# Splitting a sequence transform into even and odd tokens, on row and column tiles of TensorE

## The chip, the cores and the metric

The kernel runs on one core of one Trainium2 chip. The metric is the device time of that core in microseconds (us), the median of several executions. A profile is of one execution, and its span is 1.8 us shorter than that execution's own time (206.0 against 207.83 us in the kernel before). "The stretch" below is the time from the start of the first feed-forward matmul to the start of the last. The engines are TensorE (PE in the profile, PEld its weight loads), VectorE (DVE), ScalarE (ACT), GpSimd (POOL) and SyncE (SP). SP does no arithmetic here; it only starts the DMA transfers, and the profile calls that work SPq.

## The reference, cut to what matters

```python
B, H, S, D = 4, 8, 768, 48
def attn(r, k, v, w, u):                 # per batch and head, token by token
    for t in range(S):
        y[t]  = r[t] @ (state + outer(u * k[t], v[t]))
        state = w[t][:, None] * state + outer(k[t], v[t])

x = y.transpose(0, 2, 1, 3).reshape(4, 768, 384)
mixed = real(fft(fft(x, axis=1), axis=2))        # axis 1: tokens, axis 2: features
u  = x + mixed
un = (u - mean(u)) / sqrt(var(u) + 1e-6)         # layer norm over the features
out = u + relu(un @ w_ch1) @ w_ch2               # 384 -> 1536 -> 384
```

All inputs and the output are fp32. The change concerns the two transforms, and with them the order in which tokens lie on the partitions of the on-chip memory.

## The kernel before

The program is written as a list of operations with dependencies. A small list scheduler in the kernel file gives each engine its static order and sets the semaphores between engines. Attention works in 24 chunks (4 batches of 6) of 128 tokens; a chunk needs four loads (w, k, r, v). Each load is one DMA that puts 128 tokens on 128 partitions, in 1,024 pieces of 192 bytes (8 heads of 48 fp32 for each token):

```python
def load(b, c):
    for n in "wkrv":
        def f(e, n=n, i=i):
            return e.dma_start(INB[n][i][:, :, :],
                               src[n][b, :, c*CH:(c+1)*CH, :].rearrange("h t d -> t h d"))
        op("sp", 60, f, ..., sem="in_%s%d" % (n, i), nbytes=CH * DM * 4)
```

The first transform (over tokens) takes the sums and differences `xf` of mirrored features, and multiplies them by cosine and sine tables for 385 frequencies. The second (over features) multiplies the result by further tables. Both use the full array of 128 rows by 128 columns. A row tile is a part of this array that takes only some of the rows (input partitions), a column tile one that takes only some of the columns (output partitions); a mode change is a passage from one such division to another. The feed-forward part follows, batch by batch, while the next batches' attention runs:

```python
for s in range(NC):                      # first transform: 24 matmuls of 385 columns per batch
    e.matmul(ps(t)[:, 0:HF], xf[:, s, off:off+128], tab[:, s, :], start=a, stop=z)
...
for j in range(3):                       # second transform: 18 matmuls of 384 columns per batch
    lt = hcs[:, j, 128*kb:128*kb+128] if kb < 3 else hcr[:, j, 128*kb-S//2 : 128*kb-S//2+128]
    e.matmul(ps(t)[:, 0:DM], lt, dt[:, j, :], start=(j == 0), stop=(j == 2))
...
for q in range(HP):                      # attention product: already on two row tiles
    for x in range(2):
        e.matmul(ps(ta[x])[:, 128*q:128*q+128], kT[64*x:64*x+D, q, :], rT[64*x:64*x+D, q, :])
...
e.matmul(ps(t)[:, 0:384], W1[:, m, 128*j:128*j+128], unt[:, m, :], ...)   # feed-forward, first half
e.matmul(ps(t)[:, 0:DM], ht[:, j, 128*x:128*x+128], W2[:, j, :], ...)     # feed-forward, second half
e.dma_start(out[b, kb*128:(kb+1)*128, :], o[:, :])                        # 24 stores of 192 KB
```

## Time and profile before

| | before |
|---|---|
| median time (4 runs: 208.38 to 210.4) | 208.91 us |
| span of the profiled execution | 206.0 us |
| first feed-forward matmul | 53.9 us |
| last input landed / last attention product | 118.9 / 163 us |
| last matmul started | 202.6 us |
| TensorE busy between 53.9 and 202.9 | 148.5 of 149.0 us |

The first lines are from the page of the kernel before. Each digit of PE and DMA is the busy share of one fortieth of the span, in tenths; GB/s is what the DMA engines moved in that slice.

```profile
PE   1298887799899999999999999999999999999993
...
DMA  5999999399699999999999810011110200211202
GB/s 124 220 210 210 181 217 219 49 187 203 110 222 178 219 188 215 214 216 224 205 256 249 182 46 0 0 41 38 38 43 0 80 0 0 81 38 38 76 23 94
```

But for two dips, DMA is full until just past the middle, and TensorE is full from the twelfth slice on. Next comes the chain of waits that ended last, in shares of the span by engine.

```profile
PE 80%; DVE 8%; POOL 5%; DMA 2%; ACT 2%; issue 2%; SPq 1%; ACTq 0%; DVEq 0%; POOLq 0%
```

TensorE alone carries four fifths of it; the DMA issues (SPq) have 1%. The table of stretches (length, then each engine's busy time and number of instructions, the clock granted to TensorE, the busy share of the DMA engines, GB/s) makes the same point with numbers:

```profile
0.00:53.90 53.90, 39.91 (x405) 23.44 (x406) 43.03 (x120) 39.45 (x82) 37.90 (x49) 1.00 0.95 180
53.90:202.90 149.00, 148.53 (x1354) 94.38 (x1354) 104.24 (x228) 105.17 (x242) 71.92 (x88) 1.00 0.49 111
202.90:206.00 3.10, 0.00 (x1) 0.00 (x0) 0.62 (x1) 0.00 (x0) 0.00 (x0) 1.00 0.24 85
```

From 53.9 us on, TensorE has half a microsecond of idle time in 149. The time is therefore the start (53.9) plus what TensorE must do after it (149) plus a tail of 3 us.

Last, TensorE's timeline around an attention product (line L613) between two groups of full-array matmuls:

```profile
73.47 0.81 PE L758 MATMUL bank<-w,ht 128*128 128x384 bf16 x4
74.22 0.40 PE L613 MATMUL bank<-rtb,ktb 48*128 48x128 bf16 x8
74.54 0.34 PE L682 MATMUL bank<-ss,xf 128*128 128x385 bf16 x1
```

Four matmuls of 384 columns, 162 ns apart, would let the next one start at 74.12; it starts at 74.22. So the change from the full array to row tiles costs just under 100 ns. The records give 258 ns instead of 162 on the way in and 148 instead of 56 on the way out: 92 to 96 ns per change.

### The profile page before, as it was taken

To read this page: it belongs to the slowest core of one execution; us is meant where nothing else is said; L and a number is where in the kernel's file an instruction comes from. 1 tells how busy PE (TensorE), PEld (TensorE's weight loads), DVE (VectorE), ACT (ScalarE), POOL (GpSimd) and SP (SyncE) were. 2 spreads that over 40 slices of the span, in tenths; PEclk is the share of its full clock that TensorE was granted. 3 is DMA by queue.
4 is the path that set the end of the run, shared out by engine and by line. 5 is a ranking of instruction groups with operands and counts; after the bars stand their busy time and mean duration, and the time that the engine had idled before them with its cause. 6 is when DMAs were issued, how large, how long until landed. Compare 5 with 4: busy or idle time off the path is not lost.

```text
span 206.0 us, 4594 instructions
## 1 busy us (share of the span) xinstructions
PE 188.4 (91%) x1758; PEld 117.8 (57%) x1758; DVE 147.9 (72%) x348; ACT 144.6 (70%) x322; POOL 109.8 (53%) x136
## 2 busy tenths in 40 slices
PE   1298887799899999999999999999999999999993
PEld 0164553446565666666667666666666666665661
DVE  8917989859987878499878974999778338622222
ACT  5979987474988898868886759689963463881420
POOL 2396895779256987892798887813542130000000
PEclk9999999999999999999999999999999999999999
DMA  5999999399699999999999810011110200211202
GB/s 124 220 210 210 181 217 219 49 187 203 110 222 178 219 188 215 214 216 224 205 256 249 182 46 0 0 41 38 38 43 0 80 0 0 81 38 38 76 23 94
DMA packets 105414, 26.45 MB, mean 128 GB/s; under 512 B 100272, under 2 KB 105008, under 8 KB 105392
## 3 DMA queue, kind: packets, MB, share of 16 engines
q1 hardware_dynamic: 103440, 23.80, 53.4%
q0 software_dynamic: 1952, 2.36, 7.0%
q8 instruction: 14, 0.23, 0.4%
q14 instruction: 8, 0.07, 0.1%
HBM read 23.79 MB, written 4.72 MB: 138 GB/s over the span
## 4 chain that ended last, share of the span: by engine, by line
PE 80%; DVE 8%; POOL 5%; DMA 2%; ACT 2%; issue 2%; SPq 1%; ACTq 0%; DVEq 0%; POOLq 0%
PE bank L739 23%; PE bank L758 23%; PE bank L682 7%; PE bank L698 6%; PE bank L613 3%; POOL rk L398 2%; DMA in_v<-in_v_dram 2%; PE bank L594 2%; PE bank L715 2%; PE bank L600 2%; DVE ah L618 2%; PE bank L553 2%; PE bank L651 2%; PE bank L557 2%; PE bank L801 1%
## 5 line engine op out<-in xcount | busy, mean ns | idle before, releaser
L739 PE MATMUL bank<-unt,w 128*128 128x384 bf16 x288 | 54.8, 326 | 0.2 <-ACT unt L720 0.2
L758 PE MATMUL bank<-w,ht 128*128 128x384 bf16 x288 | 54.0, 326 | 0.0
L748 ACT ACTIVATE ht<-bank 128x384 bf16<-128x384 f32 x80 | 38.1, 490 | 17.0 <-PE bank L739 16.6
L618 DVE TENSOR_TENSOR ah<-bank,msk 128x512 bf16<-128x512 f32 x48 | 31.3, 682 | 6.2 <-PE bank L613 5.9
L758 PEld LDWEIGHTS bank<-w,ht 128*128 128x128 bf16 x288 | 26.9, 98 | 15.4
L739 PEld LDWEIGHTS bank<-unt,w 128*128 128x128 bf16 x288 | 26.2, 97 | 15.7 <-issue 0.4
L398 POOL TENSOR_TENSOR rk<-in_r,in_k 128x384 f32<-128x384 f32 x24 | 24.2, 1013 | 10.2 <-DMA in_r<-in_r_dram 9.1
L398 POOL TENSOR_TENSOR xf<-x 128x191 bf16<-128x191 f32 x18 | 11.4, 632 | 30.1 <-DVE x L657 30.1
L763 DVE SCALAR_TENSOR_TENSOR osb<-bank,rstd,uf 128x384 f32<-128x384 f32 x24 | 14.7, 614 | 17.6 <-PE bank L758 17.4
L398 POOL TENSOR_TENSOR vtd<-in_v,dc 128x384 f32<-128x384 f32 x24 | 19.9, 832 | 9.8 <-DVE dc L575 9.6
L398 POOL TENSOR_TENSOR rk<-rk,ub 128x384 f32<-128x384 f32 x24 | 24.0, 1005 | 0.3
L603 ACT ACTIVATE rtb<-bank 128x512 bf16<-128x512 bf16 x24 | 14.3, 594 | 6.8 <-PE bank L594 6.0
L412 ACT ACTIVATE un<-uf,agg 128x384 bf16<-128x384 f32 x24 | 14.2, 608 | 5.9 <-DVE agg L706 5.9
L605 ACT ACTIVATE ktb<-bank 128x512 bf16<-128x512 bf16 x24 | 14.3, 595 | 4.3 <-PE bank L600 4.1
L412 ACT ACTIVATE vb<-in_v 128x384 bf16<-128x384 f32 x24 | 12.5, 522 | 5.6 <-DMA in_v<-in_v_dram 3.0
L657 DVE TENSOR_TENSOR x<-bank,vtd 128x384 f32<-128x384 f32 x24 | 13.3, 553 | 4.4 <-PE bank L651 4.2
L744 DVE TENSOR_SCALAR ht<-bank 128x384 bf16<-128x384 f32 x16 | 8.8, 552 | 10.2 <-PE bank L739 10.2
L583 DVE TENSOR_TENSOR rh<-bank,in_r 128x384 bf16<-128x384 f32 x24 | 13.2, 551 | 3.0 <-ACT bank L559 2.7
L700 DVE TENSOR_TENSOR uf<-bank,x 128x384 f32<-128x384 f32 x24 | 12.6, 543 | 3.1 <-PE bank L698 2.8
L801 PE MATMUL bank<-idw,msk 128*128 128x384 bf16 x48 | 12.0, 353 | 3.0 <-DVE idw L402 3.0
L720 ACT ACTIVATE unt<-bank 128x384 bf16<-128x384 f32 x24 | 11.6, 491 | 4.0 <-PE bank L715 3.7
L553 PE MATMUL bank<-lb,msk 128*128 128x384 bf16 x24 | 8.2, 342 | 6.4 <-ACT lb L412 5.0
(100 smaller groups left out, 364.2 us busy)
## 6 DMA issues: line engine op xcount, KB each, us to landing
in_w<-in_w_dram SPq DMA_DIRECT2D x24, 192.0 KB, 3.8
in_k<-in_k_dram SPq DMA_DIRECT2D x24, 192.0 KB, 3.8
in_r<-in_r_dram SPq DMA_DIRECT2D x24, 192.0 KB, 3.8
in_v<-in_v_dram SPq DMA_DIRECT2D x24, 192.0 KB, 3.9
out_dram<-osb SPq DMA_DIRECT2D x24, 192.0 KB, 1.9
w<-in_moe_w_ch_dram POOLq DMA_DIRECT2D x2, 1152.0 KB, 11.7
ub<-in_u_dram SPq DMA_DIRECT2D x1, 192.0 KB, 3.8
```

The lines of the kernel that those rows point to most:

```text
L398: return shared(lambda e: e.tensor_tensor(out=o, in0=a, in1=b, op=f))
L412: return lambda e: e.activation(o, a, f, **kw)
L603: op("act", 570, lambda e: e.activation(rT[:, :, :].rearrange("p h t -> p (h t)"), psb(trr)[:, 0:512], ACTF.Copy), r=[trr], w=[("RTB", i2)])
L605: op("act", 570, lambda e: e.activation(kT[:, :, :].rearrange("p h t -> p (h t)"), psb(trk)[:, 0:512], ACTF.Copy), r=[trk], w=[("KTB", i2)])
L618: masked[n] = op("dve", 660, lambda e, x=x: e.tensor_tensor(out=ah[:, x:H:2, :], in0=ps(ta[x])[:, :].rearrange("p (h t) -> p h t", t=128), ...
L657: op("dve", 530, lambda e: e.tensor_tensor(out=xb[:, c, 0:DM], in0=ps(ty)[:, 0:DM], in1=vtd[:, :, :].rearrange("t h d -> t (h d)"), op=ALU ...
L682: return e.matmul(ps(t)[:, 0:HF], xf[:, s, off:off + 128], tab[:, s, :], start=a, stop=z)
L739: ins = e.matmul(ps(t)[:, 0:384], W1[:, m, 128 * j:128 * j + 128], unt[:, m, :], start=(m == 0), stop=(m == NM - 1))
L748: op("act", 475, lambda e, j=j, t=t, ht=ht: e.activation(ht[:, j, :], ps(t)[:, 0:384], ACTF.Relu), r=[t], w=[("HT", q % 2, j)])
L758: ins = e.matmul(ps(t)[:, 0:DM], ht[:, j, 128 * x:128 * x + 128], W2[:, j, :], start=(j == 0), stop=(j == NJ - 1))
L763: op("dve", 610, lambda e, kb=kb, t=t, o=o: e.scalar_tensor_tensor(out=o[:, :], in0=ps(t)[:, 0:DM], scalar=rstd[:, kb:kb + 1], in1=uf[:, k ...
L801: ins = e.matmul(ps(tw)[:, 0:384], MSK[:, :], IDW[:, :])
```

## The change

The transform of 768 tokens is split into even and odd tokens. Each half sum runs on half of the rows: even tokens lie on partitions 0 to 63 and odd tokens on 64 to 127, and two matmuls of 64 rows by 193 columns run side by side on two row tiles. For the frequencies k and 384 - k the two half sums are then added and subtracted. This halves the columns that TensorE streams. The price: tokens have to lie in even-odd order, so each load and each store becomes two DMAs of 64 partitions, and the second transform brings its output into the same order with column tiles. The scheduler also got new options and retuned priorities, and the two state updates of a chunk became one.

```diff
@@ load
-                return e.dma_start(INB[n][i][:, :, :],
-                                   src[n][b, :, c * CH:(c + 1) * CH, :].rearrange("h t d -> t h d"))
+                return [e.dma_start(INB[n][i][64 * x:64 * x + 64, :, :],
+                                    src[n][b, :, c * CH + x:(c + 1) * CH:2, :].rearrange("h t d -> t h d"))
+                        for x in range(2)]
@@ first transform
-                        return e.matmul(ps(t)[:, 0:HF], xf[:, s, off:off + 128], tab[:, s, :], start=a, stop=z)
+                        for x, t in enumerate((tp, tq)):
+                            pr = slice(64 * x, 64 * x + 64)
+                            ins = e.matmul(ps(t)[:, col:col + HQ], xf[pr, s, off:off + 128], tab[pr, s, :], start=a,
+                                           stop=True, skip_group_check=True)
...
-            op("act", 475, ... e.activation(hcs[:, j, :], ps(t)[:, 0:HF], ACTF.Copy) ...)
+            op("act", ...  e.activation(pc[:, 0:len(js), :], <even half sums>, ACTF.Copy) ...)
+            for x in range(2):           # on DVE: frequencies k, then 384 - k
+                    return e.tensor_tensor(out=o, in0=p, in1=q, op=ALU.subtract if x else ALU.add)
@@ second transform
-                    return e.matmul(ps(t)[:, 0:DM], lt, dt[:, j, :], start=(j == 0), stop=(j == 2))
+                    for x in range(2):
+                        if kb in (1, 4):                 # four column tiles of 32
+                            for h in range(2):
+                                ins = e.matmul(ps(t)[64 * x + 32 * h:64 * x + 32 * h + 32, 0:DM], src[:, j, o:o + 64:2],
+                                               (DTP if h and j else DTM)[:, j, :], start=(j == 0), stop=(j == 2))
+                        else:                            # two column tiles of 64
+                            ins = e.matmul(ps(t)[64 * x:64 * x + 64, 0:DM], src[:, j, o:o + 127:2],
+                                           (DTM if j == 0 or kb in (0, 3) else DTP)[:, j, :], start=(j == 0), stop=(j == 2))
@@ store
-                op("sp", 60, ... e.dma_start(out[b, kb * 128:(kb + 1) * 128, :], o[:, :]) ...)
+                    e.dma_start(out[b, kb * 128 + x:(kb + 1) * 128:2, :], o[64 * x:64 * x + 64, :]) for x in range(2)
... (tables, masks and identities for the new token order; the merged state update; scheduler options; priorities)
```

## The prediction

> **What bounds the kernel.** TensorE, from 53.9 us on. The table of stretches shows it busy 148.5 of the 149.0 us between the first feed-forward matmul (53.9) and the last (202.9); DVE, ACT and POOL are at 70, 71 and 48% there. Input DMA saturates until 118 us (slices); the last attention product runs at 163, so DMA has slack. Before 53.9 the chain of waits goes through POOL, DVE and DMA; TensorE does 8 us of filler. Behind the last matmul come 3.1 us.
>
> **What it removes.** The first transform is 24 matmuls of 385 columns per batch. The timeline gives 162 to 166 ns from start to start, 4.0 us per batch. Afterwards it is 24 pairs of 193 columns on 64 rows each. The attention product (48 rows, 128 columns) already runs on two row tiles: 8 matmuls take 4 x 56 ns, so pairs run together. A pair of 193 columns should take 83 ns: 2.0 us per batch. Saving 1.95 us per batch: 5.8 us for batches 1 to 3, which lie in the saturated stretch.
>
> **What it adds.** (1) Mode switches. At 73.5 us, four 384-column matmuls are followed by the row-tiled product 96 ns later than their columns need; after it the next full matmul starts 148 ns after the last row-tiled one instead of 56. So 92 to 96 ns per change, in either direction. This agrees with the Trainium skill, "TensorEngine Tiling (Array Packing)", Key Properties: changing the mode drains TensorE. Of the 48 changes now, 32 fall in the saturated stretch; the new order has 127, 93 of them there. 61 more x 93 ns = 5.7 us: the saving is gone, if column modes drain like row modes (no trace here shows it yet). (2) The second transform, 162 ns per step now, keeps 162 ns if two or four column tiles run together. "TensorE: Matmul & The Clock Gate", Part 3, says they do; but column tiling turns off Fast Weight Load (tiling page), which could expose weight loads: 54 steps, 0 to 60 ns each, 0 to 3 us. (3) ACT loses about 2 us, DVE gains about 4 us over the kernel (sums and differences 7, state -3); neither bounds the stretch. (4) Twice the DMA instructions, as many packets: covered by slack; last store +0.3 us.
>
> **On the critical path.** Stretch: 149.0 - 5.8 + 5.7 + about 1 = 150; if column modes do not drain, 145 to 146. Start: the ACT copy, DVE sum and reversed copy form a longer chain and DVE has 2 us more; ACT is relieved and the retuned priorities should win 1 to 3 us: feed-forward starts at 52 +- 2. Tail 3.4. Span about 204 us; timed runs are 2 to 3 us longer.
>
> **Prediction: 206.5 us, range 202 to 211.** Faster by over 2%: 0.32; within: 0.54; slower: 0.14.
>
> **What would show it.** First transform: pairs starting 3 to 4 ns apart, one pair per 83 ns (right), 160 (row tiles not concurrent). Gaps near 95 ns at each full-to-column change (right), none (then faster, about 203). Column tiles: 162 ns per step (right), over 220 (weight loads exposed). TensorE above 98% busy in the stretch. Start of feed-forward between 50 and 54.
>
> **What would make it wrong.** Column-mode changes that cost nothing; retuned start winning over 4 us; column tiles running one after the other (slower by 9 us); stride-2 input loads halving the DMA rate.

## More of the kernel before

The DMA issues of the page before read: what is moved, by which queue, how many, KB each, median us from issue to landing.

```profile
in_w<-in_w_dram SPq DMA_DIRECT2D x24, 192.0 KB, 3.8
...
out_dram<-osb SPq DMA_DIRECT2D x24, 192.0 KB, 1.9
```

And the timeline of the queue that issues them: start, duration, engine and line, what is moved.

```profile
6.54 0.76 SPq L422 DMA_DIRECT2D in_r<-in_r_dram  x1
7.34 0.82 SPq L422 DMA_DIRECT2D in_v<-in_v_dram  x1
8.20 0.93 SPq L422 DMA_DIRECT2D in_w<-in_w_dram  x1
```

A load's issue lasts 0.7 to 0.9 us here. This is not what an issue costs by itself: the transfers are the limit here, and the queue is held back: the first three loads of the run, issued before the transfers had filled up, took less (the fourth, 2.06 us). The same view at the start:

```profile
0.75 0.42 SPq L422 DMA_DIRECT2D in_w<-in_w_dram  x1
...
1.85 0.43 SPq L422 DMA_DIRECT2D in_k<-in_k_dram  x1
2.32 0.58 SPq L422 DMA_DIRECT2D in_r<-in_r_dram  x1
```

They took 0.42 to 0.58 us, and the shortest of the 96 issues took 0.37. A chunk of four loads came every 3.9 us in the median (786,432 bytes, so about 200 GB/s). Between the ninth chunk and the tenth the queue stood still for 19.5 us, waiting for the feed-forward weights.

## The result, and the profile after

| | before | after |
|---|---|---|
| median time | 208.91 us | 243.56 us (4 runs: 242.16 to 244.03) |
| span of the profiled execution | 206.0 us | 240.4 us |
| first feed-forward matmul | 53.9 us | 69.2 us |
| last input landed | 118.9 us | 164.8 us |
| last attention product | 163 us | 195.0 us |
| last matmul started | 202.6 us | 236.1 us |

The changed kernel is slower by 16%: the ratio of times is 1.163, with a 95% interval of 1.156 to 1.170. Ratios in this document are the mean time of one kernel's fast runs over that of the kernel before in the same rounds, so they are not quite the ratio of the medians quoted.

From the page of the kernel after, the slices of TensorE, of its granted clock, of the DMA engines and their rate:

```profile
PE   3358595579999998969869783999899999999993
...
PEclk9995557578999999988999997999999999999999
DMA  5888786889937787876767677675300220210214
GB/s 98 144 150 141 141 148 118 144 143 186 197 74 136 142 143 145 145 145 134 150 125 143 133 146 145 127 146 127 86 3 0 52 49 3 65 37 0 65 35 98
```

Two things differ. TensorE is no longer full in the middle of the run. And the DMA rate, which was mostly 180 to 220 GB/s while inputs came in, now stands at 133 to 150 GB/s in most slices, while the DMA engines are mostly 7 or 8 tenths busy instead of 9 or more. So something other than the DMA engines limits the transfers. The granted clock falls in the early slices in which TensorE starves; in the run with whole loads below it is 1.00 from the first feed-forward matmul to the last, so it is read here as a consequence; no run shows that alone. The chain of waits, by engine and by line, names the new limit:

```profile
PE 51%; SPq 26%; DMA 9%; DVE 9%; issue 3%; ACT 1%; DVEq 0%
SPq L442 25%; PE bank L816 15%; PE bank L835 14%; DMA out_dram<-osb 6%; PE bank L876 3%; PE bank L771 3%; PE bank L730 3%; DMA in_w<-in_w_dram 2%; PE bank L659 2%; DVE ah L664 1%; PE bank L640 1%; PE bank L766 1%; PE bank L792 1%; DVE osb L840 1%; PE bank L646 1%
```

A quarter of the span is now the issue of input loads (SPq, line L442), which had 1% before. The DMA issues and the queue's timeline show how:

```profile
in_w<-in_w_dram SPq DMA_DIRECT2D x48, 96.0 KB, 2.9
...
out_dram<-osb SPq DMA_DIRECT2D x48, 96.0 KB, 2.2
```

```profile
6.92 1.31 SPq L442 DMA_DIRECT2D in_w<-in_w_dram  x2
8.28 1.31 SPq L442 DMA_DIRECT2D in_k<-in_k_dram  x2
9.63 1.31 SPq L442 DMA_DIRECT2D in_r<-in_r_dram  x2
```

There are 48 half loads of each tensor in place of 24 whole ones, and each lands 2.9 us after its issue instead of 3.8, so a transfer does not take longer than before. The queue issues almost without pause: two half loads take 1.31 us and the next pair starts 1.35 to 1.36 us after the last. Over all 192 half loads the median issue is 635 ns, within 633 to 651 for most, plus about 42 ns between two: 677 ns for 98,304 bytes, which is 145 GB/s. That is the rate in the slices. The same number of packets of 192 bytes flowed as before (98,304), and one packet took the same time (median 15 ns in both). Where nothing else holds it back, a chunk now comes every 5.4 us (median of all: 5.6) instead of 3.9. Up to the start of the last load, at 162.1 us, the queue was issuing for 137 us; the one long pause, 15.5 us, is again the wait for the weights.

The table of stretches, and below it the sum over 100 to 160 us, which before was saturated:

```profile
0.00:69.20 69.20, 47.50 (x493) 30.06 (x494) 48.07 (x133) 36.99 (x79) 38.78 (x51) 0.78 0.80 141
69.20:236.40 167.20, 153.26 (x1523) 92.80 (x1520) 104.95 (x224) 103.37 (x237) 72.31 (x87) 0.98 0.50 98
```

```profile
sum 60.00, PE 48.21 PEld 28.47 DVE 36.40 ACT 34.87 POOL 32.69; mean PE 16.07 PEld 9.49 DVE 12.13 ACT 11.62 POOL 10.90
```

TensorE's work in the stretch is 153.3 us, and it idles for 14 us, 12 of them between 100 and 160 us. The span grew by 34.4 us: the start by 15.4, the stretch by 18.1 (148.7 to 166.8), the tail by 0.9.

What the prediction said of TensorE can be read as well. From its timeline, a change from the full array to column tiles:

```profile
209.36 0.81 PE L835 MATMUL bank<-w,ht 128*128 128x384 bf16 x4
210.10 0.68 PE L771 MATMUL bank<-dtm,hcr 128*64 128x384 bf16 x6
```

Four matmuls of 384 columns should end their slots at 210.01, and the column tiles start at 210.10: the same pause as for row tiles. The records give 255 to 259 ns instead of 162, so 93 to 97 ns, also between tiles of 64 and of 32 columns. Of the nine changes from tiles of 32 columns back to the full array, five took 268 to 271 ns, up to 109 ns of pause, and one lies in a wait.

### The profile page after: what moved, and what is told of

Read it like the earlier page. It is cut to its first block, busy times and chain, and to the rows that moved or that the text cites. A ratio compares the mean times of both kernels' runs of the same rounds, so it can differ in the third digit from the quotient of the medians.

```text
span 240.4 us, 5218 instructions
## 1 busy us (share of the span) xinstructions
PE 200.8 (84%) x2012; PEld 122.9 (51%) x2012; DVE 153.6 (64%) x357; ACT 140.4 (58%) x315; POOL 111.1 (46%) x138
## 4 chain that ended last, share of the span: by engine, by line
PE 51%; SPq 26%; DMA 9%; DVE 9%; issue 3%; ACT 1%; DVEq 0%
SPq L442 25%; PE bank L816 15%; PE bank L835 14%; DMA out_dram<-osb 6%; PE bank L876 3%; PE bank L771 3%; PE bank L730 3%; DMA in_w<-in_w_dram 2%; PE bank L659 2%; DVE ah L664 1%; PE bank L640 1%; PE bank L766 1%; PE bank L792 1%; DVE osb L840 1%; PE bank L646 1%
## 5 line engine op out<-in xcount | busy, mean ns | idle before, releaser
L835 PE MATMUL bank<-w,ht 128*128 128x384 bf16 x288 | 56.6, 336 | 0.0
L825 ACT ACTIVATE ht<-bank 128x384 bf16<-128x384 f32 x80 | 38.9, 494 | 12.9 <-PE bank L816 12.6
L418 POOL TENSOR_TENSOR kh<-in_k,e 128x384 bf16<-128x384 f32 x24 | 23.9, 1002 | 26.4 <-ACT e L611 26.4
L418 POOL TENSOR_TENSOR vtd<-in_v,dc 128x384 f32<-128x384 f32 x24 | 20.5, 858 | 14.7 <-DVE dc L620 14.7
L659 PE MATMUL bank<-rtb,ktb 48*128 48x128 bf16 x192 | 10.8, 240 | 10.3 <-ACT ktb L651 5.4
L876 PE MATMUL bank<-idb,msk 128*128 128x384 bf16 x52 | 14.1, 395 | 4.0 <-DVE idb L422 4.0
L640 PE MATMUL bank<-idb,rh 128*128 128x128 bf16 x96 | 10.7, 243 | 7.4 <-DVE rh L629 7.1
L683 DVE TENSOR_TENSOR st<-bank,e 128x384 bf16<-128x384 f32 x20 | 11.0, 551 | 8.9 <-PE bank L677 6.5
```

The source lines that it names most:

```text
L418: return shared(lambda e: e.tensor_tensor(out=o, in0=a, in1=b, op=f))
L659: ins = e.matmul(ps(ta[x])[:, 128 * q:128 * q + 128], kT[64 * x:64 * x + D, q, :], rT[64 * x:64 * x + D, q, :])
L825: op("act", 475, lambda e, j=j, t=t, ht=ht: e.activation(ht[:, j, :], ps(t)[:, 0:384], ACTF.Relu), r=[t], w=[("HT", q % 2, j)])
L835: ins = e.matmul(ps(t)[:, 0:DM], ht[:, j, 128 * x:128 * x + 128], W2[:, j, :], start=(j == 0), stop=(j == NJ - 1))
L876: ins = e.matmul(ps(tw)[:, 0:384].rearrange("p (a b) -> p a b", b=128), MSK[:, :], IDB[:, :].unsqueeze(1).to_broadcast([128, 3, 128]))
```

## The experiments

Three theories stood after this reading. A: the issue of a half load costs SP about 0.64 us, and twice the issues make the queue the limit. B: the loss is on TensorE itself (mode changes, weight loads). C: the stride of two tokens in memory makes the half loads slow. A fourth, without a letter, is that the retuned order asks for the loads later. The experiments ran in three groups, each on one chip and next to runs of the kernel before, whose medians there were 209.84, 209.69 and 208.84 us. A run without an interval is a single run.

### Whole loads in the changed kernel

The changed kernel gets back the whole loads of 128 tokens. Its results are wrong, because the partitions then hold the wrong tokens; the work of all engines is the same.

```diff
-                return [e.dma_start(INB[n][i][64 * x:64 * x + 64, :, :],
-                                    src[n][b, :, c * CH + x:(c + 1) * CH:2, :].rearrange("h t d -> t h d"))
-                        for x in range(2)]
+                return e.dma_start(INB[n][i][:, :, :],
+                                   src[n][b, :, c * CH:(c + 1) * CH, :].rearrange("h t d -> t h d"))
```

> The changed kernel with one load per tensor and chunk again (128 rows, tokens in natural order) in place of two half loads; nothing else moves, so the result is wrong on purpose (the even/odd order is lost). Theory A, the load queue is bound by its issues (two loads of 96 KB at 677 ns each give 145 GB/s, as the trace of the change shows): the input rate returns to about 205 GB/s, the last input lands near 119 us instead of 165, the first feed-forward matmul starts at 52 to 57 us instead of 69, and the time falls to 205 to 211 us. Rival B, the loss is on TensorE itself (mode drains, exposed weight loads in the column tiles): the time stays above 235 us.

Measured: 212.34 us, ratio 1.011 (1.005 to 1.016). The feed-forward started at 58.6 us, the last input landed at 128.0. The stretch is saturated again:

```profile
58.60:207.10 148.50, 148.50 (x1522) 91.45 (x1518) 105.25 (x224) 102.56 (x236) 72.36 (x87) 1.00 0.52 109
```

So the split of the loads cost 29.3 us of the 34.4 by which the span grew (240.4 to 211.1). What is left, 5.1 us, is a start 4.7 us later, a stretch 0.5 us shorter and a tail 0.9 us longer. All work of TensorE stayed, and the time did not stay above 235 us, so B falls. The time is slightly above the expected range (and the last input came 9 us later than expected), since that later start was not in it.

With the loads out of the way, this run also shows the first transform. A part of TensorE's timeline:

```profile
165.75 0.25 PE L729 MATMUL bank<-cs,xf 64*128 64x193 bf16 x2
165.84 0.24 PE L729 MATMUL bank<-ss,xf 64*128 64x193 bf16 x2
165.92 0.25 PE L729 MATMUL bank<-cs,xf 64*128 64x193 bf16 x2
```

Two row tiles start within 3 to 4 ns of each other, and most pairs follow the pair before after 82 to 84 ns. The Trainium skill, "TensorE: Matmul & The Clock Gate", Part 3, says that row tiles run together with a spacing of about 4 ns; this trace agrees.

### Half loads in the kernel before, of neighbouring tokens

The kernel before gets two DMAs of 64 partitions for each load, without any stride: tokens 0 to 63 and 64 to 127. The result is correct.

```diff
-                return e.dma_start(INB[n][i][:, :, :],
-                                   src[n][b, :, c * CH:(c + 1) * CH, :].rearrange("h t d -> t h d"))
+                return [e.dma_start(INB[n][i][64 * x:64 * x + 64, :, :],
+                                    src[n][b, :, c * CH + 64 * x:c * CH + 64 * x + 64, :].rearrange("h t d -> t h d"))
+                        for x in range(2)]
```

> The kernel before with each load split into two of 64 partitions, tokens still contiguous, same order of all other instructions; the result stays right. Theory A (issue-bound): if a half load costs the queue about 680 ns whatever its stride, the input rate falls to about 145 GB/s and the time rises to 230 to 245 us. Rival B (loss on TensorE): 209 us. Rival C (the half loads of the change are slow to issue because of their token stride of two): a contiguous half issues in under 450 ns, the rate stays above 190 GB/s and the time stays within 3% of 209 us.

Measured: 242.34 us, ratio 1.152 (1.145 to 1.160). This edit alone makes the kernel before as slow as the whole change did. Its queue:

```profile
6.87 1.31 SPq L424 DMA_DIRECT2D in_w<-in_w_dram  x2
8.23 1.31 SPq L424 DMA_DIRECT2D in_k<-in_k_dram  x2
```

These are the same 1.31 us for two half loads, with neighbouring tokens and the old schedule. So C falls, B once more, and the retuned order too. The feed-forward starts at 83.0 us and the last input lands at 160.1.

### Neighbouring tokens in the changed kernel

```diff
-                                    src[n][b, :, c * CH + x:(c + 1) * CH:2, :].rearrange("h t d -> t h d"))
+                                    src[n][b, :, c * CH + 64 * x:c * CH + 64 * x + 64, :].rearrange("h t d -> t h d"))
```

> The changed kernel with half loads that take 64 contiguous tokens instead of every second one (wrong result on purpose). Theory A with a cost per load instruction: issue stays near 635 ns and the time near 243 us. Rival C (the stride makes the issue slow): issue falls below 450 ns and the time below 215 us.

Measured, with a result that is wrong: 243.53 us (two runs), ratio 1.160 (1.151 to 1.169), 635 ns for an issue. The stride of two tokens costs nothing that can be seen:

```profile
6.93 1.31 SPq L442 DMA_DIRECT2D in_w<-in_w_dram  x2
```

### Quarter loads in the kernel before

Four DMAs of 32 partitions for each load; the diff is that of the half loads with 32 in place of 64 and `range(4)`.

> The kernel before with each load in four of 32 partitions, tokens contiguous, result right. Theory A with a cost per instruction that does not depend on its size: four issues of about 640 to 680 ns per 192 KB give about 72 to 77 GB/s, the last input lands at 250 to 280 us and the time is 290 to 340 us. If the issue cost went with the number of rows, the rate would be as with halves and the time below 250 us.

Measured in one run, correct: 290.78 us. The queue, one group of four:

```profile
7.08 1.93 SPq L424 DMA_DIRECT2D in_v<-in_v_dram  x4
```

The time fell into the range that A gave, at its lower end, but the issue did not: it took 451 ns for 32 rows and not 640. So the cost of an issue is not one fixed number. Four of them with the gaps take 1.97 us for 192 KB, about 100 GB/s. The last input landed at 214.9 us and not at 250 to 280, so the hit in time is luck.

### 112 and 16 rows

To see whether the issue time grows with the number of rows, each load was cut into 112 and 16 partitions.

```diff
-                return e.dma_start(INB[n][i][:, :, :],
-                                   src[n][b, :, c * CH:(c + 1) * CH, :].rearrange("h t d -> t h d"))
+                return [e.dma_start(INB[n][i][lo:hi, :, :],
+                                    src[n][b, :, c * CH + lo:c * CH + hi, :].rearrange("h t d -> t h d"))
+                        for lo, hi in ((0, 112), (112, 128))]
```

> The kernel before with each load in two pieces of 112 and 16 partitions, result right. Half loads cost the queue 635 ns (64 rows), quarters 451 ns (32 rows), which makes 267 ns + 5.75 ns a row; whole loads of 128 rows fall out of that line with 369 to 433 ns where nothing held them up. If the line holds for every load that is not 128 rows: 911 and 359 ns, 1.35 us per 192 KB, about 145 GB/s and 235 to 245 us. If an issue costs the same 640 ns for any part, the same rate; the two issue times tell them apart.

Measured in one run, correct: 219.11 us.

```profile
6.30 1.03 SPq L424 DMA_DIRECT2D in_w<-in_w_dram  x2
7.37 1.03 SPq L424 DMA_DIRECT2D in_k<-in_k_dram  x2
```

An issue of 112 rows took 430 ns and one of 16 rows 557 ns. The line that I had laid through the points for 32 and 64 rows (267 ns plus 5.75 ns per row) is refuted: measured are 557 ns for 16 rows, 451 for 32, 635 for 64, 430 for 112, and 0.42 to 0.58 us for 128 at the start of the kernel before. What decides it stays open. It does support A: two issues that take less time together (1.07 us a pair with the gaps, against 1.35) cost less.

### Two extra tiny issues

This run asks whether the queue's time or the transfer through 64 partitions is the limit. Whole loads stay, and each is followed by two DMAs of 64 rows by 8 bytes that nobody reads.

```diff
+                return [e.dma_start(INB[n][i][:, :, :],
+                                    src[n][b, :, c * CH:(c + 1) * CH, :].rearrange("h t d -> t h d"))] + [
+                    e.dma_start(EXTRA[n][i][64 * x:64 * x + 64, :], src[n][b, 0, c * CH:c * CH + 64, 0:2]) for x in range(2)]
```

> The kernel before with its whole loads untouched, but behind each of them two tiny loads (64 rows of 8 bytes, never read) from the same queue; result right. If the queue's issues bound the changed kernel, three issues per 192 KB (about 430 and twice about 600 ns, with the gaps 1.75 us) cap the input rate near 110 GB/s although every real load is whole: 255 to 285 us. If instead transfers of 64 partitions move their bytes more slowly, the tiny loads cost little and the time stays below 220 us.

Measured in one run, correct: 284.39 us.

```profile
7.22 0.59 SPq L426 DMA_DIRECT2D in_v<-in_v_dram  x1
7.85 1.24 SPq L428 DMA_DIRECT2D ext<-in_v_dram  x2
9.13 0.59 SPq L426 DMA_DIRECT2D in_w<-in_w_dram  x1
```

The extra transfers carry 1 KB per load next to 192 KB. Each of their issues took 596 ns and that of a whole load between them 587, in all about 1.9 us per load or 103 GB/s. So the number of issues is enough to slow the kernel by a third, and the path of the data into 64 partitions is not needed to explain it. A tiny DMA of 64 rows costs the queue nearly what one of 96 KB does. All these DMAs are issued by SP. No run issued half of the loads from another engine, so it is open whether a second queue would have given the rate back.

### No column tiles

From the run with whole loads, the second transform goes back to the full array. The results are wrong.

```diff
-                    for x in range(2):
-                        ... (two tiles of 64 or four tiles of 32 columns)
+                    ins = e.matmul(ps(t)[:, 0:DM], src[:, j, k0:k0 + 128], (DTM if j == 0 or kb < 3 else DTP)[:, j, :],
+                                   start=(j == 0), stop=(j == 2))
```

> The changed kernel with whole loads (as after_whole_loads, 212.3 us) whose second transform is again three full-array matmuls of 128 columns per output block, in place of 64- and 32-column tiles; wrong result on purpose, everything else and the order unchanged. If every change of mode costs 93 ns and a 64-column step 190 ns in place of 162, the saturated stretch loses about 3 us and the start about 1 us: 207.5 to 210 us. If the column tiles were free, 212 us.

Measured: 207.11 us, ratio 0.988 (0.983 to 0.992).

```profile
57.30:201.00 143.70, 143.61 (x1433) 93.03 (x1430) 104.53 (x224) 101.91 (x236) 73.14 (x88) 1.00 0.54 114
```

The stretch is 4.8 us shorter than with column tiles (143.4 from the first feed-forward matmul to the last, against 148.2), where I had expected about 3. With column tiles there were 93 mode changes in it, without them 48; 45 fewer at 93 to 97 ns make 4.2 to 4.4 us, an estimate from the count and the measured pause. The rest, about half a microsecond, fits the steps (a step is one group of matmuls over 384 columns, on all its tiles): 12 of the 21 steps of 64 columns that follow another took 187 to 192 ns and not 162. A weight load of 64 columns takes longer than one of 128, as the groups of weight loads show, first of the run with column tiles and then of the kernel before (busy us, mean ns of one):

```profile
L770 PEld LDWEIGHTS bank<-dtm,hcs 128*64 128x64 bf16 x32 | 1.5, 109 | 2.5 <-issue 1.6 <-DVE hcs L744 0.6
...
L770 PEld LDWEIGHTS bank<-dtp,hcs 128*64 128x64 bf16 x16 | 0.8, 111 | 0.5 <-issue 0.3
```

```profile
L698 PEld LDWEIGHTS bank<-dtm,hcs 128*128 128x128 bf16 x36 | 3.3, 98 | 2.2 <-ACT hcs L685 0.3
```

The Trainium skill, "TensorEngine Tiling (Array Packing)", Restrictions, says that column tiling turns the Fast Weight Load off; 109 to 111 ns against 98 for twice the columns agrees with it. No run shows that the slower weight loads are what lengthens the steps; those of 32 columns took 94 to 96 ns.

### The new schedule in the kernel before

The kernel before gets the scheduler options and the priorities of the change and nothing else. This asks where the later start comes from.

```diff
+    AHEAD = 0.5
+    COLD = 36000.0
+    OVER = {"dve": 70.0, "act": 95.0, "pool": 40.0}
...
-    A0, AP, F0, FL, M0, ML, P, KT, KW, DR, LT, DF = 45.4, 5.5, 26.2, 33.0, 42.6, 63.1, 43.3, 21.3, 22.7, 220.0, 143.1, 2462.0
+    A0, AP, F0, FL, M0, ML, P, KT, KW, DR, LT, DF, LA, SK, KT2, NF, W0, WP = 55.9, 4.8, 39.2, 37.2, 50.6, 61.1, 44.4, 23.5, 22.8, 208.2, 148.8, 2702.0, 0.15, 2.9, 29.6, 26.5, 2.7, 1.64
```

> The kernel before, untouched in its operations, under the new scheduler and its new priority numbers. after_whole_loads started its feed-forward 4.7 us later than before (58.6 against 53.9 us) although its loads landed as early. If the retuned schedule is the cause, this kernel starts it at 57 us or later too and takes 212 us or more; if the cause is the longer chain of copy, sum and difference and the column tiles, it starts at 52 to 55 us and takes 207 to 210 us.

Measured, correct: 208.39 us, ratio 0.995 (0.992 to 0.997); feed-forward from 54.7 us, stretch 148.3. So the retuned order explains 0.9 of the 4.7 us by which the start with whole loads is later. By one profile each, 1.2 us more belong to the column tiles (57.3 without them). For the other 2.6 us no run tells the causes apart. The longer chain behind the first transform (copy, sum, difference, reversed copy) is the likely one, but that is only argued; the clock granted before the feed-forward was also lower (0.94 with whole loads, 1.00 in the kernel before).

### The same halving without another token order

The experiments say where the change's gain lies: in the halved first transform, if it comes without split DMAs and without column tiles. The tokens s and s + 384 can be folded in place of even and odd ones. Chunk q and chunk q + 3 hold them on the same partitions, so their sum and difference are plain DVE operations. Even frequencies need only the sum, odd ones only the difference, and 24 full-array matmuls of 193 columns per batch do the work of 24 of 385. Loads, stores and second transform stay as before.

```diff
+        if q >= 0:                       # q = c - 3
+            for x in range(2):
+                op("dve", FD, tt(GX[b % 2][x][:, q, 64:448], xf[:, q, :], xf[:, c, :], ALU.subtract if x else ALU.add), ...)
...
-                        return e.matmul(ps(t)[:, 0:HF], xf[:, s, off:off + 128], tab[:, s, :], start=a, stop=z)
+                        return e.matmul(ps(t)[:, HQ * x:HQ * x + HQ], gx[x][:, q, off:off + 128], tab[:, q, x, :],
+                                        start=(q == 0 and p == 0), stop=True, skip_group_check=True)
... (tables of 3 chunks, even and odd frequencies apart; the copy puts them back in order)
```

> A version that keeps the kernel before (whole loads, natural token order, full-array matmuls) and halves the first transform otherwise: chunks 384 tokens apart are added and subtracted on DVE (6 more operations of 384 bf16 elements per batch), so that even and odd outputs are each 3 matmuls of 193 columns in place of 6 of 385. TensorE: 24 x 83 ns in place of 24 x 166 ns a batch, no mode change added: the saturated stretch loses about 5.8 us, the start 0 to 1 us (the tables are half as large). 201 to 205 us, result right. Without the gain in the stretch (DVE becoming the limit): 208 us or more.

Measured: 212.27 us, ratio 1.014 (1.010 to 1.018), and the result was wrong, with a relative error of 0.372. The flag `start` was set by the first matmul of both halves of a bank. The Trainium skill, "PSUM — Partial Sum Buffer", The four PSUM rules, says that this flag clears the accumulation bits of the whole bank. That fits: with the flag set only by the first matmul of the bank, the two runs below are correct. The stretch shrank to 145.9 us, but the feed-forward started at 62.3. I put that down to the old priorities, which let the extra DVE work delay the first batch; no run changes the priorities alone. I had expected 201 to 205 us.

The priorities were then searched again in the schedule's own bookkeeping, with the change's scheduler options and its merged state update. For a fair comparison the kernel before was searched in the same way. The second line of the diff is of the second fold; the first fold and the kernel before have other numbers in its place.

```diff
-                                        start=(q == 0 and p == 0), stop=True, skip_group_check=True)
+                                        start=(q == 0 and p == 0 and x == 0), stop=True, skip_group_check=True)
+    A0, AP, F0, FL, M0, ML, P, KT, KW, ... = 61.84, 3.29, 39.35, 34.45, 44.59, 68.65, 46.69, 73.76, 29.17, ...
```

> Control for the two runs below: the operations of the kernel before under the new scheduler, with priority numbers searched for it in the schedule's own bookkeeping for as long as for them. before_new_schedule took 208.4 us; TensorE's saturated stretch cannot shrink, only the start: 205.5 to 209 us.

> The fold of chunks 384 tokens apart, mended (only the first matmul of a bank sets start; the result is right now), with the one-piece state update of the changed kernel and the new scheduler with searched priority numbers. TensorE has 5.8 us less to do in the saturated stretch than before_retuned and no more mode changes; DVE has 9 us more for the fold over the kernel and 3 us less for the state. 201 to 205 us, 3 to 6 us below before_retuned. If DVE bounds the start instead, as in the first fold run (feed-forward only at 62.3 us): 208 us or more.

> As fold_retuned_a with another set of searched priority numbers: 201 to 206 us, result right.

| | median us | ratio (95% interval) | feed-forward from | stretch |
|---|---|---|---|---|
| kernel before, retuned | 205.78 | 0.984 (0.978 to 0.991) | 51.4 | 149.0 |
| fold, first set | 201.48 | 0.963 (0.956 to 0.970) | 52.9 | 143.6 |
| fold, second set | 200.70 | 0.959 (0.951 to 0.966) | 52.3 | 143.4 |

All three are correct; the second fold came out 0.3 us below its expected range. The stretches, first of the retuned kernel before, then of the second fold:

```profile
51.40:200.80 149.40, 148.69 (x1341) 94.20 (x1339) 106.45 (x225) 104.85 (x239) 74.83 (x90) 1.00 0.51 113
```

```profile
52.30:196.00 143.70, 143.06 (x1359) 93.64 (x1358) 111.49 (x238) 104.60 (x236) 75.84 (x91) 1.00 0.51 115
```

TensorE is full in both; the fold leaves it 5.6 us less to do, and DVE has 5 us more, which does not bound. Of the 4% that the second fold wins against the kernel before, about 1.6% is retuning (whose own interval is not clear of 2%) and the rest is the fold, with the merged state update and the luck of its own search in it. The second fold beats both the kernel before and the changed one.

One thing was not run: a single DMA that delivers the tokens in even-odd order. Whether it can be had stays open.

## Why the prediction was wrong

The prediction was 206.5 us with a range of 202 to 211; 243.56 was measured. It gave slower by over 2% a chance of 0.14.

The step that failed is the fourth added cost, in its words "Twice the DMA instructions, as many packets: covered by slack". The packets were indeed as many and as fast. But the slack was counted in the DMA engines' time and not in the issuing queue's. In the trace before, an issue lasted 0.76 us in the median, and this looked like waiting behind transfers, which it was; how long an issue lasts when nothing holds it back, and how many fit into the time, was not worked out. The kernel's own bookkeeping has the same gap: it gives 60 ns to a load (`op("sp", 60, ...)`), split or not. The sum would have been a warning: with the 0.42 to 0.58 us of the first loads, 192 issues take 81 to 111 us, about the 94 us that 24 chunks at 3.9 us took, so little or no room was left. With the measured 677 ns it is 130 us. The 44 us between the last input and the last attention product did not cover this: the last input came 46.0 us later, the last product 32 us later, and TensorE starved in between. The runs showed 29.3 us of the 34.4 us of span there.

- "feed-forward starts at 52 +- 2" was wrong, at 69.2. With whole loads it is 58.6, so 10.6 us of the miss are the loads' and 6.6 us the change's own. The retuned priorities won nothing at the start (54.7 in the kernel before).
- "Stride-2 input loads halving the DMA rate" stood among what would make the prediction wrong. The place was right and the mechanism wrong: the rate fell from about 200 to 145 GB/s, and neighbouring tokens gave the same 635 ns.
- The saving of the first transform was right. Pairs start 3 to 4 ns apart and a pair takes 82 to 84 ns (predicted 83). In the stretch, 72 matmuls at 165 ns, 11.9 us, became 72 pairs at 85 ns on average, 6.1 us: 5.8 saved, as predicted. (Waits and pauses at mode changes are left out of both.)
- The mode changes were right in number and size: about 61 more in the stretch, most at 92 to 97 ns each, for columns as for rows. The Trainium skill, "TensorEngine Tiling (Array Packing)", Key Properties, says that changing the mode drains TensorE; this trace agrees.
- The column steps were about right: 162 or 188 ns for 64 columns, which makes about half a microsecond, inside "0 to 3 us".
- The sum for the stretch was therefore close: 150 us predicted, 148.2 measured with whole loads. TensorE's own part of the change came out even, as predicted; what decided the time was outside TensorE.
- The tail was predicted 0.3 us longer and became 0.9 us longer. The half stores take a median of 597 ns to issue, each, against 332 for a whole store.

## What to carry to other kernels

Before splitting DMAs, count the instructions on the issuing queue as well as the bytes: find in the trace an issue that nothing holds back, multiply it by the new number of issues, and compare this with the time in which the data must arrive. Then measure one issue of the new shape before trusting the product: here the issues of whole loads at the start (0.42 to 0.58 us) were still below the 0.635 us of the half loads. An issue that waits behind full DMA engines looks like slack and tells nothing of what a smaller one will cost. When an algebraic saving asks for a new data order, look for another form of it that keeps the order: here the fold of tokens half a sequence apart gave the same saving on TensorE without a split transfer and without a mode change.

## What the Trainium skill lacked or had wrong

- "DMA: Bandwidth & Descriptors", Issuing engines are not separate DMA queues (not wrong): it says of the time that the sequencer takes to initiate a DMA that it "is usually small relative to the DMA itself". Here it was 635 ns for each load of 96 KB, plus 42 ns to the next, while 96 KB at the 200 GB/s of the kernel before take 0.49 us. The issue was the limit.
- I found on no page how long an issue takes by shape. The runs show 430 ns for 112 rows of 8 pieces of 192 bytes, 635 for 64, 451 for 32 and 557 for 16, and 596 for 64 rows of one piece of 8 bytes. A whole load of 128 rows took 0.42 to 0.58 us at the start of the kernel before and 587 ns between tiny ones. It doesn't rise with rows or bytes, and what it depends on stays open.
- "TensorEngine Tiling (Array Packing)", Key Properties: it has the drain at a mode change, but no size. The runs show 92 to 97 ns for most changes, into and out of row tiles and column tiles, and between column tiles of 64 and of 32; out of tiles of 32 columns up to 110.
- "TensorEngine Tiling (Array Packing)", Restrictions: it says that column tiling turns the Fast Weight Load off, but not there what that costs a step. A weight load of 64 columns took 109 to 111 ns on average against 98 for 128 columns, and 12 of 21 steps on tiles of 64 columns took 187 to 192 ns and not 162; that the one causes the other is not shown.
